# Attention with a bilinear feed-forward block on one core: a quarter of the exponentials moved from ScalarE to VectorE and GpSimd

## The chip, the cores and the metric

The kernel runs on one core of one Trainium2 chip. The metric is the device time of one execution in microseconds (us). Every kernel was executed several times. An execution counts as fast when it lies within 1.5% of the fastest one of its kernel, and only fast ones are compared. The profile gives the mean clock granted to TensorE as a share of full speed; it is shown beside the times where it matters.

The engines are named as in the profile: PE is TensorE (PEld its weight loads), ACT is ScalarE, DVE is VectorE, POOL is GpSimd.

## The reference

For x of 2048 rows and 512 columns, the kernel computes an attention block of 32 heads of 16 columns, a bilinear feed-forward block (no nonlinearity) of width 1376, and mixes them row by row with a sigmoid gate:

```python
g = sigmoid((x * gate_w).sum(-1, keepdims=True))
q, k, v = split_heads(x @ wqkv)                    # 32 heads of 16
p = softmax((q @ k.T) * 16 ** -0.5)                # 32 x 2048 x 2048
a = merge_heads(p @ v) @ wo
b = ((x @ w_gate) * (x @ w_up)) @ w_down
out = g * a + (1 - g) * b
```

(Abridged; the data are bf16.) The softmax has 32 x 2048 x 2048 exponentials, which are 2048 tiles of 128 keys by 512 queries. They are the bulk of the work outside TensorE. No maximum is subtracted: the scores are small.

## The kernel before

Scores are computed transposed, keys on partitions. Four heads share the array in a row of 32-row tiles; ScalarE takes the exponential of three tiles (1536 columns) in one instruction, and writes bf16 to a ring `PT`. The values have a column of ones beside them, so that P.V also yields the softmax's denominator.

```python
def scores(i):                     # up to 3 tiles of 128 keys x 512 queries
    ...
    r = pe.matmul(psS[:, lo : lo + 512],
                  KE[32 * j : 32 * j + 32, p, b, kt * 128 : (kt + 1) * 128],
                  QT[32 * j : 32 * j + 32, c % 2, b, :],
                  start=True, stop=True, tile_position=(32 * j, 0))
    ...
def exp(i):                        # every exponential of the kernel is here
    ...
    a.activation(PT[:, r0 : r0 + n, :].rearrange("p a b -> p (a b)"),
                 psS[:, slot[i] : slot[i] + 512 * n], ACT.Exp, scale=0.25)
    ...
def pv(e):                         # 4 heads of one key tile, 4 column tiles of the array
    ...
    for j in range(4):
        r = pe.matmul(psO[32 * j : 32 * j + 32, :], Vp[:, kt, 8 * b + 2 * j + p, :],
                      PT[:, cell[4 * e + j], :], start=(kt == 0), stop=(kt == T - 1),
                      tile_position=(0, 32 * j), skip_group_check=True)
    ...
```

(Projections, feed-forward matmuls and the output product are fed in between as TensorE has room, their evictions run on VectorE, and GpSimd multiplies the result by the reciprocal of the denominator.)

The softmax here doesn't subtract the row's maximum and nothing guards it: scores larger than these inputs give would overflow.

## Time and profile before

| | before |
|---|---|
| time, median of 2 (range) | 1001.39 us (997.35 to 1005.44) |
| span of the profiled execution | 998.0 us |
| ScalarE busy | 939.2 us, 94% |
| TensorE busy, mean granted clock | 786.5 us, 79%; 0.838 |
| VectorE busy | 159.1 us, 16% |
| GpSimd busy | 50.3 us, 5% |

From the profile page of the kernel before: the busy times, the busy tenths of TensorE and ScalarE with the granted clock (40 slices of 25 us), the chain of waits, and three groups of instructions (line, engine, operation, output and inputs, count; then busy us and mean ns of one; then the idle time ahead of them and who ended it).

```profile
PE 786.5 (79%) x5072; PEld 187.9 (19%) x5072; DVE 159.1 (16%) x260; ACT 939.2 (94%) x713; POOL 50.3 (5%) x41
...
PE   3787788888888787788877788778778777777797
...
ACT  2677799999999999999999999999999999999998
...
PEclk9998899999997999998999999998557955555557
...
ACT 61%; issue 17%; PE 14%; DVE 4%; DMA 2%; SPq 0%; ACTq 0%; DVEq 0%
...
L541 ACT ACTIVATE PT<-psS 128x1536 bf16<-128x1536 f32 (+1 forms) x694 | 925.0, 1657 | 47.6 <-PE psS L520 47.1
L520 PE MATMUL psS<-QT,KE 32*128 32x512 bf16 x2048 | 319.4, 455 | 156.3 <-ACT PT L541 144.0
...
L617 POOL TENSOR_TENSOR OT<-oraw,rb 128x512 bf16<-128x512 f32 x31 | 39.2, 1266 | 909.1 <-DMA rb<-rscr 909.1
```

ScalarE's row is at 9 from the sixth slice to the last but one: it is the bound, and its one big group (L541, 694 instructions, 925 us) is nearly all of it. Between the first exponential at 19.6 us and the end of the last at 981.4 us it hardly waits: the 47.6 us of the row include 14.0 us of waiting ahead of the first one, so 33.6 us lie between. VectorE and GpSimd have room. The last row tells something else: from about 700 us on, where the feed-forward work has run out, the clock of TensorE is at half for most of the time.

From the table by stretches of the kernel before: us, busy time (and instructions) of TensorE, its weight loads, VectorE, ScalarE and GpSimd, then the granted clock.

```profile
500.00:550.00 50.00, 38.30 (x272) 10.28 (x272) 6.99 (x12) 50.00 (x39) 1.60 (x2) 1.00 0.06 20
...
800.00:850.00 50.00, 38.05 (x226) 7.17 (x226) 1.89 (x4) 50.00 (x39) 2.53 (x2) 0.50 0.04 12
```

ScalarE is busy for all of both stretches, at clock 1.00 and at 0.50: it has no use for TensorE's speed as long as the scores come in time.

### The profile page before, as it was taken

Reading aid. Unit: us, or ns where it says so; the run is one execution under the profiler, and the core shown is the slowest. Engines: PE = TensorE matmul, PEld = TensorE weight load, DVE = VectorE, ACT = ScalarE, POOL = GpSimd, SP = SyncE. Lnnn points to the kernel's source line nnn. Section 1 sums busy time; section 2 is a strip of 40 time slices with the busy share of each in tenths; the row PEclk is TensorE's granted clock in tenths of the full one; section 3 lists DMA queues with packets and bytes.
Section 4 is the critical chain, followed back from the end, with each engine's and each line's share of the span. In section 5 each row is a group of like instructions: output and inputs, shape, how many; then the busy total and the mean of one; then the engine's idle time right before and its main releaser. Section 6 shows DMA issues by size and latency. Waiting matters only on the chain.

```text
span 998.0 us, 11864 instructions
## 1 busy us (share of the span) xinstructions
PE 786.5 (79%) x5072; PEld 187.9 (19%) x5072; DVE 159.1 (16%) x260; ACT 939.2 (94%) x713; POOL 50.3 (5%) x41
## 2 busy tenths in 40 slices
PE   3787788888888787788877788778778777777797
PEld 0222122222222222222212122121111111111111
DVE  1333332122211111111011112110000100000001
ACT  2677799999999999999999999999999999999998
POOL 4000000000000000000000000000000000000000
PEclk9998899999997999998999999998557955555557
DMA  7600000000000000000000000000000000000000
GB/s 147 191 12 1 12 12 11 3 11 12 12 12 23 22 4 9 12 12 12 13 12 22 12 11 12 12 12 12 1 11 17 28 12 12 12 1 11 12 12 21
DMA packets 29980, 19.91 MB, mean 20 GB/s; under 512 B 19464, under 2 KB 24936, under 8 KB 29928
## 3 DMA queue, kind: packets, MB, share of 16 engines
q1 hardware_dynamic: 26760, 17.59, 6.2%
q10 hardware_dynamic: 3168, 1.57, 0.8%
q8 instruction: 39, 0.64, 0.3%
q14 instruction: 13, 0.11, 0.0%
HBM read 14.45 MB, written 2.35 MB: 17 GB/s over the span
## 4 chain that ended last, share of the span: by engine, by line
ACT 61%; issue 17%; PE 14%; DVE 4%; DMA 2%; SPq 0%; ACTq 0%; DVEq 0%
ACT PT L541 60%; PE psS L520 4%; PE psO L563 3%; DVE KE L275 2%; PE psF L263 2%; PE psF L304 2%; DVE Vp L309 1%; DMA den<-oraw 1%; PE psF L350 1%; DMA xT<-in_A_x_dram 1%; PE psF L393 1%; PE psF L286 1%; PE psF L432 1%; ACT L718 1%; ACT L717 1%
## 5 line engine op out<-in xcount | busy, mean ns | idle before, releaser
L541 ACT ACTIVATE PT<-psS 128x1536 bf16<-128x1536 f32 (+1 forms) x694 | 925.0, 1657 | 47.6 <-PE psS L520 47.1
L520 PE MATMUL psS<-QT,KE 32*128 32x512 bf16 x2048 | 319.4, 455 | 156.3 <-ACT PT L541 144.0
L563 PE MATMUL psO<-PT,Vp 128*32 128x512 bf16 x2048 | 241.1, 461 | 5.1 <-DVE Vp L309 4.8
L520 PEld LDWEIGHTS psS<-QT,KE 32*128 32x128 bf16 x2048 | 69.2, 93 | 459.5 <-ACT PT L541 418.7
L617 POOL TENSOR_TENSOR OT<-oraw,rb 128x512 bf16<-128x512 f32 x31 | 39.2, 1266 | 909.1 <-DMA rb<-rscr 909.1
L563 PEld LDWEIGHTS psO<-PT,Vp 128*32 128x32 bf16 x2048 | 54.0, 95 | 157.5 <-issue 143.0
L350 PE MATMUL psF<-xT,wu 128*128 128x512 bf16 (+1 forms) x176 | 61.0, 408 | 9.2 <-DVE hT L381 7.4
L393 PE MATMUL psF<-wd,hT 128*128 128x512 bf16 (+1 forms) x176 | 62.9, 408 | 1.2 <-DVE bsb L399 1.1
L369 PE MATMUL psF<-xT,wg 128*128 128x512 bf16 (+1 forms) x176 | 58.8, 394 | 3.1 <-DVE usb L360 1.9
L595 DVE COPY oraw<-psO 128x512 f32<-128x512 f32 x31 | 21.4, 692 | 227.5 <-PE psO L563 227.2
L360 DVE CAST usb<-psF 128x512 bf16<-128x512 f32 (+1 forms) x44 | 30.2, 687 | 109.8 <-PE psF L350 109.8
L381 DVE TENSOR_TENSOR hT<-psF,usb 128x512 bf16<-128x512 f32 (+1 forms) x44 | 30.1, 684 | 96.1 <-PE psF L369 96.1
L263 PE MATMUL psF<-xT,wk 128*128 128x512 bf16 x64 | 22.0, 442 | 22.9 <-DMA xT<-in_A_x_dram 12.8
L432 PE MATMUL psF<-wo,OT 128*128 128x512 bf16 x96 | 36.2, 419 | 0.7 <-DVE ost L415 0.7
L399 DVE TENSOR_SCALAR bsb<-psF,omg 128x512 bf16<-128x512 f32 x16 | 11.9, 745 | 114.3 <-PE psF L393 114.3
L275 DVE TENSOR_SCALAR KE<-psF,mask 128x512 bf16<-128x512 f32 x32 | 22.5, 744 | 39.9 <-PE psF L263 39.9
L286 PE MATMUL psF<-xT,wq 128*128 128x512 bf16 x64 | 22.9, 426 | 3.1 <-DVE KE L275 2.4
L415 DVE SCALAR_TENSOR_TENSOR ost<-psF,gval,bsb 128x512 bf16<-128x512 f32 x13 | 9.8, 751 | 92.7 <-PE psF L432 87.6
L304 PE MATMUL psF<-wv,xT 128*128 128x512 bf16 x64 | 17.8, 403 | 2.1 <-DVE KE L275 1.4
L350 PEld LDWEIGHTS psF<-xT,wu 128*128 128x128 bf16 (+1 forms) x176 | 12.3, 100 | 38.0 <-issue 19.3
L393 PEld LDWEIGHTS psF<-wd,hT 128*128 128x128 bf16 (+1 forms) x176 | 13.0, 97 | 32.4 <-issue 27.2
L369 PEld LDWEIGHTS psF<-xT,wg 128*128 128x128 bf16 (+1 forms) x176 | 12.3, 99 | 30.6 <-issue 17.9
(42 smaller groups left out, 109.8 us busy)
## 6 DMA issues: line engine op xcount, KB each, us to landing
rb<-rscr SPq DMA_DIRECT2D x31, 256.0 KB
out_dram<-ost SPq DMA_DIRECT2D x16, 128.0 KB, 1.7
wu<-in_B_w_up_dram SPq DMA_DIRECT2D x1, 1376.0 KB, 6.4
wg<-in_B_w_gate_dram SPq DMA_DIRECT2D x1, 1376.0 KB, 9.3
wd<-in_B_w_down_dram SPq DMA_DIRECT2D x1, 1280.0 KB, 12.4
wv<-in_A_wqkv_dram ACTq DMA_DIRECT2D x1, 512.0 KB, 6.4
wo<-in_A_wo_dram SPq DMA_DIRECT2D x8, 64.0 KB, 7.9
den<-oraw SPq DMA_DIRECT2D x31, 8.0 KB
```

The source lines that it names most:

```text
L263: return pe.matmul(psF[:], wk[:, kt, b * 128 : (b + 1) * 128], xT[:, kt, ch * 512 : (ch + 1) * 512], start=s0, stop=s1,)
L275: lambda v, p=p: v.tensor_scalar(KE[:, p, b, ch * 512 : (ch + 1) * 512], psF[:], mask[:, p : p + 1], None, ALU.mult),
L286: return pe.matmul(psF[:], wq[:, kt, b * 128 : (b + 1) * 128], xT[:, kt, c * 512 : (c + 1) * 512], start=s0, stop=s1,)
L304: return pe.matmul(psF[:], xT[:, kt, t * 128 : (t + 1) * 128], wv[:, kt, :], start=s0, stop=s1)
L350: return pe.matmul(psF[0:w, :], wu[:, kt, f * 128 : f * 128 + w], xT[:, kt, c * 512 : (c + 1) * 512], start=s0, stop=s1,)
L369: return pe.matmul(psF[0:w, :], wg[:, kt, f * 128 : f * 128 + w], xT[:, kt, c * 512 : (c + 1) * 512], start=s0, stop=s1,)
L393: return pe.matmul(psF[:], hT[0:w, f, tt * 128 : (tt + 1) * 128], wd[0:w, f, :], start=s0, stop=s1)
L432: return pe.matmul(psF[:], OT[:, (NQ * c + g) % NOT, tt * 128 : (tt + 1) * 128], wo[:, g, :], start=s0, stop=s1)
L520: r = pe.matmul(psS[:, lo : lo + 512], KE[32 * j : 32 * j + 32, p, b, kt * 128 : (kt + 1) * 128], QT[32 * j : 32 * j + 32, c % 2, b, :], s ...
L541: lambda a: a.activation(PT[:, r0 : r0 + n, :].rearrange("p a b -> p (a b)"), psS[:, slot[i] : slot[i] + 512 * n], ACT.Exp, scale=0.25,),
L563: r = pe.matmul(psO[32 * j : 32 * j + 32, :], Vp[:, kt, 8 * b + 2 * j + p, :], PT[:, cell[4 * e + j], :], start=(kt == 0), stop=(kt == T - 1),
L617: lambda g: g.tensor_tensor(OT[:, m % NOT, :], oraw[:, s, :], rb[:, s, :], ALU.mult),
```

## The change

The intent is to take a quarter of ScalarE's work away. Of the four heads of each key tile, one (j = kt mod 4, called a D tile here) is no longer exponentiated by ScalarE. Queries are scaled so that a score arrives as 128 log2(e) s, where s is the scaled score. Adding a constant and converting to int16 then gives the bit pattern of a bf16 number near e^s: the integer part of log2 lands in the exponent, and the fraction is used as mantissa, a linear interpolation of the power of two. To bring its error down, the kernel averages four such interpolations, shifted against each other by a quarter of an octave: the same pattern plus 0, 32, 64 and 96. The shifts are undone by weights in the stationary operand (`VD` holds the values times 0.84, 0.71 and 0.59), and P.V adds all four up.

So a D tile costs: one PSUM-to-int16 instruction on VectorE, three int16 "shift copies" from SBUF to SBUF, made for two tiles at a time (1024 columns) by VectorE or GpSimd, whichever the builder picks, and four times the P.V work. And the order of all engines is no longer written by hand: a greedy event model at build time keeps a clock for every engine, gives each instruction a duration, and emits what is ready first. In the built program every engine runs its list in that order; semaphores keep the dependences.

The core of the diff (cut; it replaces nearly the whole schedule, about 1,650 changed lines):

```diff
-                lambda a: a.activation(
-                    PT[:, r0 : r0 + n, :].rearrange("p a b -> p (a b)"),
-                    psS[:, slot[i] : slot[i] + 512 * n],
-                    ACT.Exp, scale=0.25,
-                ),
+                lambda a: a.activation(cell_ap(c, n), src, ACT.Exp, scale=LN2 / 128.0),     # 3 heads of 4
...
+            add("dve", [sc],                                                                 # the 4th head
+                lambda v: v.tensor_scalar(cell_ap(pr["cell"] + i, 1, mybir.dt.int16), bk.ap, CB, 0.0, ALU.add, ALU.max),
+                0.61, prio=0, cb=cb, alloc=al)
...
+        def try_copy(eng, t):                          # called for "dve" and for "pool"
+            ...
+                if eng == "pool":
+                    k = pr["k"][-1]
+                else:
+                    k = pr["k"][0]
+                    if k == 3 and clock["pool"] < t + 0.5:
+                        continue
+            ...
+            if eng == "dve":
+                fn = lambda v: v.tensor_single_scalar(cell_ap(c, n, I16), cell_ap(pr["cell"], n, I16), 32.0 * k, ALU.add)
+                occ = 0.07 + 0.133 * n
+            else:
+                fn = lambda g: g.tensor_scalar(cell_ap(c, n, I16), cell_ap(pr["cell"], n, I16), 32.0 * k, 1.0, ALU.add, ALU.mult)
+                occ = 0.16 + 0.50 * n
...
+                    r = e.matmul(psO[32 * j : 32 * j + VW, :], pv_stationary(m, kt, j, k), cell_ap(cell, 1),
+                                 start=s0, stop=s1, tile_position=(0, 32 * j), skip_group_check=True)
...
+        f0, f1 = 100.0, 1470.0                         # where the feed-forward work is spread
```

The scores of D tiles go mostly to a PSUM bank of their own, `psX`. And all 128-column matmuls are cut into four of 32 columns, so that they and P.V use one tiling of the array.

## The prediction

> **What bounds the kernel now.** ScalarE: the page's first part has it busy 939 of 998 us (94%); the chain of waits gives it 61%; the table by stretches has it 97 to 100% busy from 100 us on. It exponentiates 2048 score tiles (128x512), mostly three at a time; the timeline shows one such instruction every 1.34 us. About 20 us pass before the first and 17 us after the last. VectorE is 16% busy, GpSimd 5%. When the feed-forward work runs out near 700 us, the granted clock falls from 0.95 to 0.5 without hurting ScalarE.
>
> **What the change moves** (counts from the order of the built program):
> - ScalarE keeps 1536 tiles, mostly in pairs: 658 of two, 73 of three. A pair is about 0.92 us ([...]pairs late in the old trace average 0.94): 703 us, against 932.
> - VectorE gets 512 PSUM-to-int16 instructions, estimated 0.62 us (isolated 128x512 evictions show 0.69, the second of a close pair 0.66): 317 us. And 453 SBUF shift copies of 1024 elements[...]. With its evictions (140 us), about 610 us.
> - GpSimd gets 315 such copies. Its two-input 128x512 multiply takes 1.27 us; one input at half the cost per element gives an estimated 1.2 us: 380 us, with the rest 430 us.
> - TensorE: P.V grows from 512 to 896 groups of four, scores go in 732 groups, the other matmuls are cut into four of 32 columns so that P.V and they share one tiling. The timeline shows 0.21 us between groups of one tiling, 0.32 across a change of tiling. [...]1316 changes x 0.11, V and gate: about 680 us at full clock. The feed-forward is spread over nearly the whole run: I expect the clock above 0.9.
>
> **Critical path.** Almost all of ScalarE's 230 us lie on it. But TensorE (680) is now as long as ScalarE (703), in a fixed order, so stalls add up. The order's event model knows no contention between VectorE and GpSimd[...].
>
> **Sum.** 10 us start (x transposed on TensorE, not by DMA), 17 us tail, 740 to 800 between: **800 us**, range 745 to 865. Faster by over 2%: 0.96; within 2%: 0.02; slower: 0.02.
>
> **What will show it.** ScalarE busy about 700 us, 88% of the span, waiting for scores over 47 us; VectorE 600 to 760 us; the mean shift copy near 0.4 us means no lock, over 0.6 us the lock; GpSimd copies near 1.2 us; clock over 0.9 in the last quarter too; a chain split among ScalarE, TensorE and VectorE.
>
> **What would make it wrong.** Faster: no lock. Slower: GpSimd copies well above 1.2 us, [...]four-column groups issuing slower than 0.21 us, or the clock falling to 0.5, which makes TensorE the bound at over 1000 us.

Passages of the records that no trace or run of this case shows are cut here and in the expectations below, and the cuts are marked. The 740 to 800 us between and the **800 us** in all were made with the cut terms in them. Cut are: the step from three tiles to two in the length of a pair, about 0.92 us (in the trace of the kernel before, pairs start 0.917 us apart in the mean); the length of one VectorE shift copy and the sum for 453 of them, which with 317 and 140 us made up VectorE's about 610 us; the time of a group in TensorE's about 680 us (at 0.215 us, the least between the starts of two 512-column matmuls in that trace, 732 + 924 + 716 groups are 510 us, and the 1316 changes of tiling are 145 us); and a passage by which a VectorE copy and a GpSimd instruction hold each other up, called the lock from here on. Its term took VectorE to 760 us, past ScalarE. The start of 10 us was the author's estimate. Measured since are the int16 instruction, 0.679 us for the 0.62 estimated, and the rest under "Why the prediction was right or wrong".

## The result and the profile after

The changed kernel takes 905.02 us (median of 2, 900.75 to 909.3) against 1001.39 us. Ratios in this document are made from runs of both kernels in the same rounds; they are not quite the ratio of the times quoted (here 905.02 over 1001.39 would be 0.9038): here 0.9017, with a 95% interval of 0.886 to 0.9174. It is faster, as predicted, but 105 us slower than predicted and outside the range.

| | before | after | predicted |
|---|---|---|---|
| time | 1001.39 | 905.02 | 800 |
| ScalarE: exponentials | 925.0 | 721.4 | 703 |
| ScalarE: idle before exponentials | 47.6 | 152.9 | over 47 |
| VectorE busy | 159.1 | 768.0 | 600 to 760 |
| GpSimd busy | 50.3 | 415.7 | about 430 |
| TensorE busy | 786.5 | 765.7 | about 680 (issue time) |
| mean granted clock | 0.838 | 0.944 | over 0.9 |

From the profile page of the kernel after, the lines that answer to those above:

```profile
PE 765.7 (84%) x9718; PEld 217.2 (24%) x9718; DVE 768.0 (85%) x1229; ACT 736.5 (81%) x753; POOL 415.7 (46%) x406
...
PE   7998977887888888888989887888987887788995
...
DVE  2988787987869999999898898799979998897784
ACT  3988865966759999899787795899968898688884
...
PEclk9997799999999999999987799699999999999897
...
DVE 6%; PE 4%; ACT 2%; issue 0%; POOL 0%; ACTq 0%
...
L1302 ACT ACTIVATE PT<-psS 128x1024 bf16<-128x1024 f32 (+1 forms) x732 | 721.4, 1090 | 152.9 <-PE psS L823 136.5
L922 POOL TENSOR_SCALAR PT<-PT 128x1024 int16<-128x1024 int16 x315 | 356.7, 1143 | 401.7 <-DVE PT L877 248.5
L919 DVE TENSOR_SCALAR PT<-PT 128x1024 int16<-128x1024 int16 x453 | 319.1, 735 | 10.8 <-PE psO L979 2.4
...
L877 DVE TENSOR_SCALAR PT<-psX 128x512 int16<-128x512 f32 x324 | 220.0, 679 | 56.9 <-PE psS L823 47.8
```

No row is at 9 throughout any more. ScalarE (81%), TensorE (84%) and VectorE (85%) are all near the top and none is at it. The clock stays up to the end. The chain of waits can be followed back through 12% of the span only, so it cannot name a bound here.

From the totals of waits of the kernel after (who waited, for whom: us in total, times, longest):

```profile
POOL PT L922 <- DVE PT L877: 248.5, 126, 16.4
ACT PT L1302 <- PE psS L823: 136.5, 117, 11.6
PEld psX L823 <- DVE PT L877: 115.7, 172, 1.9
...
PE psX L823 <- DVE PT L877: 34.7, 60, 1.4
```

ScalarE waits for scores (136.5 us), and the scores of D tiles wait for VectorE to have read the bank `psX` (the two lines of psX). From the instructions of the line of VectorE's shift copies, in the kernel after (count, minimum, median and maximum ns):

```profile
L919 DVE TENSOR_SCALAR PT<-PT x453: 355/583/1500, 23.6 to 888.5; 128x1024 int16<-128x1024 int16 x151
```

The same instruction on the same size takes between 0.355 and 1.5 us, 0.735 us in the mean. Sorted by what GpSimd was doing: of the 453 copies, 83 meet no GpSimd instruction, and have a mean of 0.410 us; 370 overlap one, with a mean of 0.808 us. 268 start while a GpSimd instruction is running, and 240 of those end within 0.277 to 0.282 us after the end of that instruction. That is how a lock looks: the blocked copy does not run more slowly, it is held until the other engine is done. (It does not start anew: 0.28 us is less than the shortest copy, 0.355 us, so a part of the copy's time passes while it is held.)

One such chain in the timeline of the kernel after (start, duration, engine, line, operation; a number in front of an arrow is the idle time and the arrow what ended it):

```profile
499.05 2.22 POOL L922 TENSOR_SCALAR PT<-PT 128x1024 int16<-128x1024 int16 x2
...
499.40 2.13 DVE L919 TENSOR_SCALAR PT<-PT 128x1024 int16<-128x1024 int16 x2
...
501.46 0.73 DVE L732 SCALAR_TENSOR_TENSOR ost<-psS,gval,bsb 128x512 bf16<-128x512 f32 x1
502.12 0.67 DVE L877 TENSOR_SCALAR PT<-psX 128x512 int16<-128x512 f32 x1
...
502.85 0.09 PEld L823 LDWEIGHTS psX<-QM,KE 32*128 32x128 bf16 x1 [1.45 <-DVE PT L877]
...
502.85 0.38 PE L823 MATMUL psX<-QM,KE 32*128 32x512 bf16 x1 [0.95 <-DVE PT L877]
...
503.30 1.45 ACT L1302 ACTIVATE PT<-psS 128x1536 bf16<-128x1536 f32 x1 [0.62 <-PE psS L823]
```

Two VectorE copies, which would take 0.8 us unhindered, take 2.13 us beside two GpSimd copies. The output combination (L732) and then the int16 instruction (L877) come late behind them, the bank `psX` comes free at 502.8, TensorE's next score group, which holds scores for ScalarE too, has idled for it (0.95 us of the array), and ScalarE starts its next exponential after 0.62 us of idling. The lock is between VectorE and GpSimd, but three in-order queues hand it on to ScalarE.

In the span of 907.3 us, the first exponential starts at 17.2 us and the last ends at 883.1 us: 17.2 of start, 866.0 between, 24.1 of tail. The prediction had 10, about 773, and 17.

### The profile page after: what moved, and what is told of

Its sections match the earlier page's. It is cut to its first block, busy times and chain, and to the rows that moved or that the text cites. A ratio compares the mean times of both kernels' runs of the same rounds, so it can differ in the third digit from the quotient of the medians.

```text
span 907.3 us, 22838 instructions
## 1 busy us (share of the span) xinstructions
PE 765.7 (84%) x9718; PEld 217.2 (24%) x9718; DVE 768.0 (85%) x1229; ACT 736.5 (81%) x753; POOL 415.7 (46%) x406
## 5 line engine op out<-in xcount | busy, mean ns | idle before, releaser
L1302 ACT ACTIVATE PT<-psS 128x1024 bf16<-128x1024 f32 (+1 forms) x732 | 721.4, 1090 | 152.9 <-PE psS L823 136.5
L922 POOL TENSOR_SCALAR PT<-PT 128x1024 int16<-128x1024 int16 x315 | 356.7, 1143 | 401.7 <-DVE PT L877 248.5
L919 DVE TENSOR_SCALAR PT<-PT 128x1024 int16<-128x1024 int16 x453 | 319.1, 735 | 10.8 <-PE psO L979 2.4
L823 PE MATMUL psS<-QM,KE 32*128 32x512 bf16 x1724 | 297.5, 403 | 29.7 <-ACT PT L1302 17.5
L979 PE MATMUL psO<-PT,VS 128*18 128x512 bf16 x2048 | 274.8, 401 | 14.6 <-DVE oraw L1016 8.4
L877 DVE TENSOR_SCALAR PT<-psX 128x512 int16<-128x512 f32 x324 | 220.0, 679 | 56.9 <-PE psS L823 47.8
L979 PE MATMUL psO<-PT,VD 128*18 128x512 bf16 x1536 | 242.5, 401 | 16.0 <-DVE PT L919 9.5
L823 PE MATMUL psX<-QM,KE 32*128 32x512 bf16 x324 | 130.4, 402 | 55.8 <-DVE PT L877 34.7
L877 DVE TENSOR_SCALAR PT<-psS 128x512 int16<-128x512 f32 x188 | 126.7, 677 | 5.0 <-PE psS L823 4.9
L823 PEld LDWEIGHTS psS<-QM,KE 32*128 32x128 bf16 x1724 | 70.3, 91 | 193.8 <-ACT PT L1302 97.1
```

Source lines behind the costliest of these rows:

```text
L823: r = e.matmul(bk.ap, KE[32 * j : 32 * j + 32, b, kt * 128 : (kt + 1) * 128], QM[32 * j : 32 * j + 32, p, b, :], start=True, stop=True, ti ...
L877: lambda v: v.tensor_scalar(cell_ap(pr["cell"] + i, 1, mybir.dt.int16), bk.ap, CB, 0.0, ALU.add, ALU.max),
L919: fn = lambda v: v.tensor_single_scalar(cell_ap(c, n, I16), cell_ap(pr["cell"], n, I16), 32.0 * k, ALU.add)
L922: fn = lambda g: g.tensor_scalar(cell_ap(c, n, I16), cell_ap(pr["cell"], n, I16), 32.0 * k, 1.0, ALU.add, ALU.mult)
L979: r = e.matmul(psO[32 * j : 32 * j + VW, :], pv_stationary(m, kt, j, k), cell_ap(cell, 1), start=s0, stop=s1, tile_position=(0, 32 * j), s ...
L1302: lambda a: a.activation(cell_ap(c, n), src, ACT.Exp, scale=LN2 / 128.0),
```

## The experiments

The theory going in is the lock theory: the lock makes VectorE late, and its lateness passes through TensorE to ScalarE. Its first rival is the TensorE theory: TensorE's own list, with its groups and its changes of tiling, is the bound and would be so without the lock. A second rival is that VectorE's sheer load is the bound, lock or not. Each expectation quoted below says itself what each theory expects. All fifteen runs were made beside runs of the kernel before on the same chip. Six are wrong in their results, because work was cut out or added without adjusting the rest; they are marked. All others are correct.

### The changed kernel again, as a control

> The changed kernel again, as it is, so that the others can be set beside it on the same chip. Expected 895 to 915 us, mean shift copy on VectorE 0.70 to 0.77 us, VectorE busy 755 to 780 us.

Measured 899.26 us (891.14 to 900.98), ratio 0.8968 [0.8908, 0.9028]. The first result is repeated.

### GpSimd's copies made short, order unchanged (wrong)

```diff
-  fn = lambda g: g.tensor_scalar(cell_ap(c, n, I16), cell_ap(pr["cell"], n, I16), 32.0 * k, 1.0, ALU.add, ALU.mult)
+  fn = lambda g: g.tensor_scalar(cell_ap(c, n, I16)[:, 0:16], cell_ap(pr["cell"], n, I16)[:, 0:16], 32.0 * k, 1.0, ALU.add, ALU.mult)
   occ = 0.16 + 0.50 * n
```

(And a memset of the cells at the start, so that nothing is read that was never written.) The model still believes the old duration, so all lists keep their order.

> Order of every engine unchanged; each GpSimd shift copy handles 16 columns in place of 1024 (wrong result on purpose)[...]. Theory A (the lock between VectorE and GpSimd, passed on through the fixed order, costs about 80 us): the mean VectorE shift copy falls from 0.74 to 0.36 to 0.45 us, VectorE busy from 768 to about 620 us, time to 815 to 845 us. Theory B (the order is bound by TensorE and ScalarE anyway and the lock only fills VectorE's slack): VectorE busy falls as much, but the time stays at 885 us or more.

Measured 829.56 us (827.65 to 833.23), ratio 0.8292 [0.8246, 0.8339], 70 us below the control. From its profile page:

```profile
ACT 62%; PE 26%; DVE 8%; issue 2%; DMA 1%; SPq 1%; POOL 0%; ACTq 0%; POOLq 0%; DVEq 0%
...
L1308 ACT ACTIVATE PT<-psS 128x1024 bf16<-128x1024 f32 (+1 forms) x732 | 707.0, 1169 | 86.8 <-PE psS L829 77.2
...
L925 DVE TENSOR_SCALAR PT<-PT 128x1024 int16<-128x1024 int16 x453 | 190.5, 451 | 10.9 <-PE psO L985 2.5
L928 POOL TENSOR_SCALAR PT<-PT 128x16 int16<-128x16 int16 x315 | 85.8, 277 | 538.3 <-DVE PT L883 299.2
```

VectorE's copies fall from 0.735 to 0.451 us, ScalarE's idle time from 152.9 to 86.8 us, which is 66 of the 82 us by which the profiled span fell (907.3 to 825.7). The edit takes away GpSimd's own duration together with the lock, and no run takes away the lock alone in this order. In the kernel after, TensorE's P.V (weight loads and matmuls together) waits for GpSimd's cells for 15.0 us only, 22 times, and neither VectorE nor ScalarE shows a wait for them; so I put most of the gain down to the lock, by this argument. Between the first and the last exponential there are now 787.2 us: inside the 740 to 800 of the prediction. So without the lock and with short GpSimd copies the middle of the sum would have been about right, and the lock theory holds for this order. What remains, 86.8 us of idling, is mostly not the lock (a copy that meets no GpSimd instruction takes 0.417 us here, against the mean of 0.451). The chain of waits, which broke off after 12% of the span in the kernel after, can now be followed over nearly all of it: VectorE is 8% of it, TensorE 26%, ScalarE 62% (first line above).

An example of the remainder in this kernel's timeline:

```profile
107.48 1.05 PE L477 MATMUL psX<-xT,wg 128*32 128x512 bf16 x16 [0.93 <-DVE PT L883]
...
109.34 1.05 PE L477 MATMUL psX<-xT,wk 128*32 128x512 bf16 x16 [0.17 <-DVE hT L685]
110.44 0.69 DVE L506 CAST KE<-psX 128x512 bf16<-128x512 f32 x1 [1.15 <-PE psX L477]
...
111.19 0.38 PE L829 MATMUL psX<-QM,KE 32*128 32x512 bf16 x1 [0.80 <-DVE KE L506]
...
111.64 1.02 ACT L1308 ACTIVATE PT<-psS 128x1024 bf16<-128x1024 f32 x1 [4.44 <-PE psS L829]
```

The keys of the next block of heads (xT times wk) are projected at 109.34, behind feed-forward work (wg), cast by VectorE at 110.44, and only then can the first scores be made: ScalarE has been idle for 4.44 us. As I read it, the order makes them just in time, and the chip is a little later than the model.

### No copies by GpSimd at all

```diff
         def try_copy(eng, t):
+            if eng == "pool":
+                return None
             best = None
-                    if k == 3 and clock["pool"] < t + 0.5:
-                        continue
```

> GpSimd makes no shift copies; VectorE makes all 768 (right result, order made anew by the same model). Theory A: VectorE busy falls to 710 to 735 us although it does 315 copies more, mean shift copy 0.36 to 0.45 us, and the time is 860 to 900 us, at or below the changed kernel's. Theory B (GpSimd's 315 copies are real help): VectorE becomes the bound, busy 800 us or more, time 930 us or more.

Measured 899.7 us (891.14 to 904.17), ratio 0.8969 [0.8891, 0.9047]: the same as the control. Its page:

```profile
ACT 44%; PE 31%; DVE 21%; issue 2%; DMA 1%; SPq 1%; ACTq 0%; DVEq 0%
...
L1302 ACT ACTIVATE PT<-psS 128x1024 bf16<-128x1024 f32 (+1 forms) x745 | 712.4, 1123 | 152.5 <-PE psS L823 132.4
...
L919 DVE TENSOR_SCALAR PT<-PT 128x1024 int16<-128x1024 int16 x768 | 294.5, 431 | 8.5 <-PE psO L979 3.8
```

The lock is all but gone (0.431 us a copy; 36 of the 768 still overlap one of the few GpSimd instructions left), but 768 copies instead of 453 bring VectorE to 740.3 us, near the 768.0 of the control, and ScalarE idles just as long. This corrects the lock theory: the lock is not special. A VectorE that is busy for 740 us with unblocked copies, in a fixed order beside two engines of 727 and 768 us, costs as much as a locked one. It speaks for the theory of VectorE's load, and so does the chain of waits (first line), in which VectorE has 21%, against 8% with the short GpSimd copies. (The order was made anew here, so it is not the control's.)

### A model that knows the lock

```diff
+            if task.eng == "pool" or task.prio == 99:      # prio 99: a shift copy
+                PORT[0] = t + task.occ
...
         def try_copy(eng, t):
+            if PORT[0] > t:
+                return None
```

(And GpSimd takes the shift by 96 of every pair, VectorE the other two; and small relaxations, so that the model does not get stuck.)

> The same work, but the build-time model knows that a VectorE shift copy and any GpSimd instruction exclude each other, GpSimd takes one of the three copies of each pair and VectorE two (right result). Theory A: mean VectorE shift copy under 0.5 us, VectorE busy 630 to 690 us, ScalarE's wait for scores under 100 us, time 835 to 875 us. Theory B: time 890 us or more in spite of the shorter copies.

(What the model is told is what the trace of the kernel after shows: 218 of the 232 VectorE copies that start inside a GpSimd copy, and 22 of the 36 that start inside another GpSimd instruction, end 0.277 to 0.282 us after it.)

Measured 891.19 us (886.68 to 892.44), ratio 0.8896 [0.8846, 0.8945]. The expectation of a clear gain failed. From its page:

```profile
L931 DVE TENSOR_SCALAR PT<-PT 128x1024 int16<-128x1024 int16 x512 | 288.5, 605 | 10.5 <-PE psO L991 6.0
```

The mean of a copy is 0.605 us, and 280 of 512 copies still overlap a GpSimd instruction. The model separates the two engines in its own time, but nothing on the chip makes them keep that time: they drift, and meet. The model's durations were off too (0.336 us for a free copy, which measured 0.412); a model with the right ones was not tried. Here, at least, a static order without waits did not keep the two engines apart.

### Short feed-forward streams (wrong)

The base is the run with short GpSimd copies; the feed-forward matmuls stream 64 of 512 columns.

```diff
-  bk.ap, wu[:, kt, f * 128 : f * 128 + w], xT[:, kt, c * 512 : (c + 1) * 512], kt == 0, kt == KD - 1
+  bk.ap[:, 0:64], wu[:, kt, f * 128 : f * 128 + w], xT[:, kt, c * 512 : c * 512 + 64], kt == 0, kt == KD - 1
```

(The same for wg and wd.)

> On top of e1 (small GpSimd copies, 829.6 us), the order still unchanged: the feed-forward matmuls stream 64 columns in place of 512[...] (wrong result on purpose). Theory T (what keeps e1 at 830 us, 100 us over the 730 of ScalarE's own work with start and tail, is TensorE's load): 770 to 795 us. Theory V (it is VectorE's load): 815 us or more. Theory O (it is the fixed order's chain of waits itself, no engine's load): 815 us or more here and in e5 alike.

Measured 863.02 us (851.99 to 868.8), ratio 0.8567 [0.8481, 0.8654]: slower than its base by some 30 us, though TensorE has less to do. The mean clock fell from 0.974 to 0.860. From its table by stretches (the column before the last two is the clock):

```profile
475.00:525.00 50.00, 42.70 (x537) 11.63 (x535) 42.34 (x81) 49.06 (x53) 9.09 (x22) 0.97 0.09 28
525.00:575.00 50.00, 42.93 (x474) 10.38 (x470) 37.27 (x71) 40.57 (x42) 5.91 (x18) 0.73 0.05 13
```

Where the clock is 0.97 ScalarE is busy for 49.06 of 50 us; where it is 0.73, for 40.57. The second stretch has no idle gap of TensorE above 0.86 us, so no long gap goes with its low clock. (The two stretches lie in different parts of the work, so their difference is not the clock's alone: in the base, ScalarE was busy for 41.36 and 47.22 us of the same two stretches of time, at clocks of 0.91 and 0.95.) The kernel before has a low clock without a long gap too: between 800 and 850 us no gap was longer than 0.74 us, TensorE was busy for 38.05 of 50 us, and the clock was 0.50; between 500 and 550 us it was busy for as long, 38.30 us, and the clock was 1.00. This run tells nothing about TensorE's load at a constant clock, and the theories it should have told apart are untouched by it. It does suggest that ScalarE now depends on the clock, which it did not before the change: the clock is the only thing that this edit made worse.

### Short shift copies on VectorE too (wrong)

```diff
-  fn = lambda v: v.tensor_single_scalar(cell_ap(c, n, I16), cell_ap(pr["cell"], n, I16), 32.0 * k, ALU.add)
+  fn = lambda v: v.tensor_single_scalar(cell_ap(c, n, I16)[:, 0:16], cell_ap(pr["cell"], n, I16)[:, 0:16], 32.0 * k, ALU.add)
```

> On top of e1, the order unchanged, TensorE's load as in the changed kernel: VectorE's 453 shift copies too handle 16 columns in place of 1024 (wrong result on purpose), which takes about 140 us off VectorE (649 to about 510 us busy). Theory V: 770 to 795 us. Theory T: 815 us or more. Theory O: 815 us or more.

Measured 824.46 us (820.87 to 830.96), ratio 0.8239 [0.8187, 0.8292]. VectorE's busy time falls by 102 us, from 649.3 to 547.5, and the time by 5. With the lock gone, at 650 us, VectorE is no longer what holds the others.

### Both together (wrong)

The edits of the two runs above, together.

> e4 and e5 together. Theories T and V: if loads are all there is, 740 to 770 us, near ScalarE's 703 us with 27 us of start and tail. Theory O: 800 us or more, because the order itself makes ScalarE wait for projections that are issued just before they are needed.

Measured 849.69 us (847.95 to 857.63), ratio 0.85 [0.8446, 0.8553], at a clock of 0.876. As with the short streams alone, the clock confounds it, and I read nothing from it beyond a second sight of the clock falling.

### Copies from a base tile with a pitch

The base tile is stored in 33 pieces of 32 with a pitch of 34, and the copies are contiguous with 1056 columns. The run asks whether the lock hangs on this access pattern.

```diff
+ def odd_ap(c, base):
+     a = PD[:, (c - RA) // 2, :].bitcast(mybir.dt.int16)
+     return a.rearrange("p (r w) -> p r w", w=34)[:, :, 0:32] if base else a[:, 0:1056].rearrange("p (r w) -> p r w", w=32)
...
-                    if k == 3 and clock["pool"] < t + 0.5:
+                    if k == 2 and clock["pool"] < t + 0.8 or k == 3 and clock["pool"] < t + 1.0:
                         continue
...
-  fn = lambda v: v.tensor_single_scalar(cell_ap(c, n, I16), cell_ap(pr["cell"], n, I16), 32.0 * k, ALU.add)
-  occ = 0.07 + 0.133 * n
+  fn = lambda v: v.tensor_single_scalar(odd_ap(c, False), odd_ap(pr["cell"], True), 32.0 * k, ALU.add)
+  occ = 0.62
```

(Three cells fewer, for space. The second part gives GpSimd more of the copies. Not shown: one more setting of the builder, the threshold `fp` below which P.V is used as filler, went from 2 to 4.)

> Right result, candidate: VectorE's shift copies read 33 pieces of 32 elements with gaps and write 1056 elements in one run[...]. GpSimd makes most of the copies, VectorE the rest, order made anew with 0.62 us a VectorE copy. [...]VectorE copies 0.60 to 0.75 us with almost no spread and no tie to GpSimd's ends, VectorE busy 640 to 690 us, time 840 to 875 us. If any VectorE access to SBUF beside GpSimd locks: spread as before (0.6 to 1.7 us), time 890 us or more.[...]

(The first set of figures is for a lock that hangs on the access pattern.)

Measured 865.2 us (862.97 to 870.57), ratio 0.8647 [0.8596, 0.8697], correct. From the instructions of its copy line:

```profile
L936 DVE TENSOR_SCALAR PD<-PD x307: 641/695/706, 20.3 to 841.7; 128x1056 int16<-128x1056 int16 x154
```

The copy is slower than an unblocked one (0.410 us in the mean), and nearly always the same: 0.641 to 0.706 us, though 213 of the 307 start while a GpSimd instruction runs. GpSimd's copies are steady too (1.041 to 1.059 us, against 1.039 to 1.327 in the kernel after). There is no lock left; that the lock hangs on the access pattern is shown by the run further down that restores it in an unchanged order. The gain on the control is 34 us, but this order also gives GpSimd more of the copies (461 instead of 315), and a run below, with only such a sharing and the lock left in, gains as much. So this run shows the lock off, and does not show that taking it away pays.

### The same with four settings of the builder changed

```diff
-                    if k == 2 and clock["pool"] < t + 0.8 or k == 3 and clock["pool"] < t + 1.0:
+                    if k == 2 and clock["pool"] < t + 1.2 or k == 3 and clock["pool"] < t + 1.0:
-        f0, f1 = 100.0, 1470.0
+        f0, f1 = 240.0, 1500.0
-                if lag >= 3:
+                if lag >= 4:
-                    if bk is s[2] and (third or lag < 3 or (st["mq"] and bk is DB)):
+                    if bk is s[2] and (third or lag < 4 or (st["mq"] and bk is DB)):
-            if nfree < 6 or fp < 4 or st["ua"] >= NA:
+            if nfree < 6 or fp < 5 or st["ua"] >= NA:
```

That is: still more copies to GpSimd; the feed-forward work starts later, away from the stretch where projections of keys and values are needed; D tiles may lag a little more; P.V is used as filler sooner when cells run short. (The duration that the model gives a VectorE copy also went from 0.62 to 0.63 us.)

> Right result, candidate: e7 with the build-time order made with other settings (GpSimd does two of three shift copies more strictly, feed-forward work starts at ScalarE unit 240 in place of 100, incomplete groups of P.V are allowed earlier). No lock remains, so the order should hold on the chip as it did for e1 and e7: 815 to 845 us, VectorE copies 0.70 us without spread, GpSimd busy 640 to 690 us. If TensorE's clock or load is the bound, it stays within 1% of e7 (857 to 873 us).

Measured **814.02 us** (812.04 to 821.61), ratio 0.8118 [0.8076, 0.8159], correct: the best of all, ahead of both kernels. Its page:

```profile
PE 740.0 (91%) x9718; PEld 225.8 (28%) x9718; DVE 637.4 (79%) x1029; ACT 722.3 (89%) x749; POOL 583.5 (72%) x607
...
PEclk8999989999999999999999999999999999999998
...
L1319 ACT ACTIVATE PT<-psS 128x1024 bf16<-128x1024 f32 (+1 forms) x728 | 707.3, 1142 | 66.8 <-PE psS L840 39.2
```

ScalarE is up to 89%, its idle time down to 66.8 us, VectorE at 637.4 us, GpSimd at 583.5. The time is a little under what was expected, and GpSimd was to be busy for 640 to 690 us. That the gain on the run before is 51 us speaks against TensorE's load or clock as the bound there, by the expectation's own test. What the parts are worth is asked by the last four runs below.

### More work for TensorE (wrong)

On the run with short GpSimd copies, one further matmul of 256 columns after each of the 734 score groups, which writes values that are there already.

```diff
-                return r
+                return e.matmul(
+                    bk.ap[:, 0:256],
+                    KE[32 * j : 32 * j + 32, b, kt * 128 : (kt + 1) * 128],
+                    QM[32 * j : 32 * j + 32, p, b, 0:256],
+                    start=True, stop=True, tile_position=(32 * j, 0),
+                )
```

> On top of e1, order unchanged: each of the 732 score groups is followed by one more matmul of 256 columns that writes the same values again (harmless), an estimated 0.11 us or more each, 80 us in all, on TensorE alone. Theory T (without the lock TensorE's time is the bound): 890 us or more, that is nearly all of it is added to e1's 830. Theory O (the fixed order's chains; TensorE has slack): 830 to 860 us.

Measured 871.82 us (855.52 to 884.79). Only two executions are fast, 855.52 and 867.37 us; the two others, at 876 and 885 us, are counted as slow. The ratio, 0.8679 [0.8625, 0.8734], does not fit the two fast ones, whose mean over that of the kernel before in these rounds (1003.6) is 0.858; it fits the median of all four. In the timeline the next group comes 0.42 us after a score group instead of 0.32, so 734 x 0.10 = 73 us were added to TensorE's list. The mean of the fast executions rose from 830.0 to 861.4 us, by 31 us; set against the kernel before on each chip (0.858 against 0.829) by some 28 us. With the slow ones counted it would be 42 us (medians). So roughly 30 to 40 us, about half of what was added, with only two fast executions behind it. It lies between what the two theories expected. TensorE's list is not all of the critical path, but much of it.

### Less work for ScalarE (wrong)

On the same base, ScalarE exponentiates 256 of every 512 columns.

```diff
-            src = bass.AP(lo.tensor, lo.offset, [list(lo.ap[0]), [1, 512 * n]])
+            src = bass.AP(lo.tensor, lo.offset, [list(lo.ap[0]), [512, n], [1, 256]])
-                lambda a: a.activation(cell_ap(c, n), src, ACT.Exp, scale=LN2 / 128.0),
+                lambda a: a.activation(PT[:, c : c + n, 0:256], src, ACT.Exp, scale=LN2 / 128.0),
```

> On top of e1, order unchanged: ScalarE exponentiates 256 of every 512 columns (wrong result on purpose), which takes about 300 us of work off ScalarE[...]. Theory T: 770 us or more, because TensorE's own time stays. If ScalarE were still the bound: under 700 us.

Measured 790.49 us (783.59 to 797.18), ratio 0.7847 [0.7802, 0.7892]. From its page:

```profile
PE 714.5 (91%) x9718; PEld 211.8 (27%) x9718; DVE 645.1 (83%) x1230; ACT 461.9 (59%) x753; POOL 155.3 (20%) x407
...
L1313 ACT ACTIVATE PT<-psS 128x512 bf16<-128x512 f32 (+1 forms) x732 | 446.8, 618 | 302.5 <-PE psS L834 282.9
```

ScalarE's busy time fell by 260 us, from 722.1 to 461.9, and the time by 39 to 42 us (45 by the ratios, 0.7847 against 0.8292). The rest turned into idling, 302.5 us of it, 282.9 of them for scores. With ScalarE at 59% the kernel still takes about 790 us: I take that to be TensorE's list (714.5 us busy, 91%) with the waits it has for evictions, copies and projections. ScalarE's 722 us and this floor of about 790 lie close together, which would explain why neither TensorE's added 73 us nor ScalarE's removed 260 us show fully.

### The best order with contiguous copies again

The same order as the best version, but base and copies contiguous and 1024 wide, as in the changed kernel, to see whether the lock comes back.

```diff
-  return a.rearrange("p (r w) -> p r w", w=34)[:, :, 0:32] if base else a[:, 0:1056].rearrange("p (r w) -> p r w", w=32)
+  return a[:, 0:1024]
```

(And the base cell's layout to fit.)

> e8 with one thing undone: the same order of every engine, the same cells, but the shift copies read and write 1024 elements in one run again[...]. [...]unblocked VectorE copies 0.41 us in place of 0.70, blocked ones end 0.28 us after the GpSimd instruction, mean 0.75 to 1.0 us since GpSimd is busy 72% of the time; time 840 to 885 us against e8's 814. If e8's gain over the changed kernel came from its order alone: 800 to 820 us.

(The first set of figures is for the lock coming back.)

Measured 825.11 us (819.46 to 828.78), ratio 0.8213 [0.8155, 0.8271]: 11 us slower than the best version by the medians; the intervals of the two ratios overlap by a hair (0.8159 and 0.8155), so the size of it is not firm. The time lies between the two expectations. From the instructions of its copy line:

```profile
L935 DVE TENSOR_SCALAR PD<-PD x253: 386/593/1376, 22.1 to 801.9; 128x1024 int16<-128x1024 int16 x127
```

The lock is back: 0.386, 0.593 and 1.376 us (minimum, median, maximum), a mean of 0.727, GpSimd's copies up from 1.044 to 1.110 us. In this order contiguous copies cost about 11 us more than copies with the pitch. This is not the price of the lock alone: the nine copies that meet no GpSimd instruction take 0.424 us, less than the 0.698 us of a copy with the pitch, so here the lock and the faster copy nearly cancel. With 253 VectorE copies, at 0.727 against 0.698 us, VectorE's sum rises by 8 us only, from 637.4 to 645.8. As I read it, the lock's price is what it adds to an engine that others wait for; it is not a constant.

### More copies to GpSimd, and the other settings, one by one

So two things besides the lock made the best version. On the changed kernel, with its contiguous copies and the lock: (1) only the rule that shares the copies; (2) only the other settings (f0 and f1, the two lags, the filler threshold); (3) both.

```diff
-                    if k == 3 and clock["pool"] < t + 0.5:
+                    if k == 2 and clock["pool"] < t + 1.2 or k == 3 and clock["pool"] < t + 1.0:
                         continue
```

> The changed kernel with one rule of its model altered: GpSimd gets about two of three shift copies (about 507) and VectorE one (about 261); all else as it was[...] (right result, order made anew). Theory L (what the lock costs depends on how many VectorE copies meet it and on VectorE's load): VectorE busy falls from 764 to 640 to 670 us, time 840 to 865 us. Theory R (only the order's other settings matter): 885 us or more.

> The changed kernel with only e8's other settings: feed-forward from unit 240 to 1500, thresholds 4 and 5 for third banks and for incomplete P.V groups; shift copies shared as in the changed kernel (453 and 315)[...] (right result). Theory L: VectorE busy stays at 755 us or more and the time at 865 to 890 us. Theory R: 815 to 845 us.

> e12 and e13 together, with [...]the changed kernel's 46 cells (right result): 810 to 835 us if the two add up.

| | old settings | new settings |
|---|---|---|
| old sharing (453 copies on VectorE, 315 on GpSimd) | 899.26 (control) | 884.55 [0.8757, 0.8884] |
| new sharing (about 260 and 507) | 865.08 [0.856, 0.8673] | 833.43 [0.8231, 0.8349] |

(Medians in us; in brackets the interval of the ratio to the kernel before. The control ran on another chip, where the kernel before took 999.18 instead of 1003.74 us.) Sharing alone is worth 34 us, the settings alone 15, both 66 (35, 15 and 68 by the ratios). From the page of the run with the new sharing alone:

```profile
L919 DVE TENSOR_SCALAR PT<-PT 128x1024 int16<-128x1024 int16 x261 | 191.6, 741 | 11.4 <-PE psO L979 1.3
```

A VectorE copy still takes 0.741 us, as locked as ever; there are fewer of them, and VectorE's busy time falls from 768 to 655 us. So the cheap cure here is to let GpSimd, which was 46% busy, do more, in spite of the lock. Why both together give 17 us more than their sum is not settled.

### The runs against VectorE's load

| run | VectorE busy | ScalarE idle before exponentials | time |
|---|---|---|---|
| settings only | 770.2 | 135.3 | 884.55 |
| changed kernel | 768.0 | 152.9 | 905.02 (control 899.26) |
| no GpSimd copies | 740.3 | 152.5 | 899.7 |
| lock in the model | 739.6 | 144.5 | 891.19 |
| copies with the pitch | 670.0 | 118.7 | 865.2 |
| sharing only | 654.9 | 116.3 | 865.08 |
| sharing and settings | 653.0 | 81.9 | 833.43 |
| short GpSimd copies | 649.3 | 86.8 | 829.56 |
| best order, contiguous copies | 645.8 | 78.2 | 825.11 |
| best version | 637.4 | 66.8 | 814.02 |
| short copies on both | 547.5 | 84.6 | 824.46 |

(The runs that changed TensorE's or ScalarE's work are left out.) From 770 down to about 650 us the time falls with VectorE's load on the whole (not in every step: the settings alone, at 770 us, beat the run without GpSimd copies, at 740), whether that load is lock, number of copies or slower copies. These are different orders, so the table shows that the two go together, not that one makes the other; only three pairs keep one order (768 and 649, 649 and 548, 637 and 646). Below 650 us, 102 us less load gave 5 us. The load is not all: among the four runs between 645 and 655 us, the one with the old settings and full GpSimd copies takes 865 us, the one with the old settings and short ones 830. With full copies, the settings are worth about 30 us there.

## Why the prediction was right or wrong

- **What bounds before:** right. ScalarE was the bound, and taking a quarter of its tiles gave the direction.
- **ScalarE's new work:** nearly right, 721 us for 703.
- **The lock:** right. The trace after shows it, with 240 of 268 copies ending 0.277 to 0.282 us after the GpSimd instruction that they started in. The mean shift copy was put over 0.6 us with the lock and near 0.4 without; it was 0.735, and 0.410 for the copies that met no GpSimd instruction. VectorE was put at up to 760 us; it was 768.0.
- **The length of a free copy:** too short, and not taken from a trace. The free ones took 0.410 us in the mean, 0.355 to 0.428.
- **GpSimd's copies:** right, 1.143 us for 1.2 (1.046 for the 41 that overlap no shift copy of VectorE). That one input costs half as much per element was the author's estimate; here 1024 elements of one input took 1.046 us, and 512 of two inputs 1.266 (L617, before).
- **TensorE's groups:** right. In the timeline of the kernel after, groups follow at 0.22 us in one tiling (500.42 to 500.64) and at 0.32 across a change (500.10 to 500.42), as read from the trace before: a change of tiling costs about 0.1 us.
- **The clock:** right, 0.944, and up to the last quarter.
- **What will show it:** ScalarE was busy 81% of the span, not 88%; a chain split among three engines could not be seen, since the chain of waits ends after 12% of the span.
- **The sum: this is the step that failed.** "10 us start ..., 17 us tail, 740 to 800 between". In the span of 907.3 us the terms measured 17.2, 24.1 and 866.0. The ends account for 14 of the 107 us; ScalarE's own work for 18 (721 for 703); and the waits between exponentials for the remaining 75 (866.0 - 721.4 = 145, where 773 - 703 = 70 had been allowed).

Why this term was too small: I charged the lock to VectorE's busy time, noted that VectorE would then be longer than ScalarE, and then took the longest engine plus some stalls as the length of the middle. On the chip the lateness is handed on, VectorE to `psX`, `psX` to TensorE's in-order list, that list to ScalarE. ScalarE waits while VectorE works, and VectorE waits elsewhere for TensorE, so the sum is well past the longest of the three. With the lock taken out of the same order, together with the length of GpSimd's copies, the middle was 787.2 us, within the predicted 740 to 800; the two together were worth about 70 us of time in this order, and by the 15 us of waits for GpSimd's cells most of it was the lock. I had counted it in full in VectorE's time, and as next to nothing of the kernel's. The span of that run, 825.7 us, is 26 us over the prediction: 12 at the ends (15.7 + 22.8 against 27) and 14 in the middle.

The first form of my theory, that the lock as such is the cause, fell as well: the version without GpSimd copies has next to no lock, and the same time. In this order the lock is, for the most part, what makes VectorE late; in the other orders tried it is VectorE's load, of which the lock is one part, together with the order around it. Once VectorE is relieved, TensorE's list is what ScalarE waits for: 260 us less of ScalarE's work gave about 40, 73 us more of TensorE's cost some 30 to 40, 102 us less of VectorE's gave 5.

What stays open: how the 87 us of ScalarE's idling that remain with short GpSimd copies (7 of them ahead of the first exponential) divide among just-in-time projections, changes of tiling and dips of the clock. The run that should have told (short feed-forward streams) was spoiled by the clock. Also why sharing and settings together give more than their sum, and why full GpSimd copies at a like VectorE load cost 35 us against short ones under the old settings: this leaves room for GpSimd's own duration as a cause beside the lock, which only a run with the lock gone and full copies in the old order would tell.

## What to carry to other kernels

When a change brings the bound engine down to the level of two others, in fixed in-order lists, do not predict the longest of the three plus a little: what makes one of them late can be paid by all. Nor does such a lateness have one price: short GpSimd copies, and with them almost no lock, gained 70 us in one order, and going back from copies with a pitch to contiguous ones cost 11 us in another. Here it paid to give the copies to the engine that had time, even where it contended, and so to take load off the engine that frees the buffers; then see which engine's relief still moves the time. An order that was planned at build time did not keep two engines apart without waits (280 of 512 copies still met), so either count the contention as load or choose an access pattern that does not contend (here the pitch: 0.641 to 0.706 us a copy, against 0.355 to 1.500).
